# Filter pieces on GpSimd's queue and a first transform with eight column groups ahead, in a frequency filter followed by a SiLU layer

## Chip, core and metric

The kernel runs on one core of one Trainium2 chip. The metric is the device time of one execution in microseconds (us); all times below are in us unless marked ns. An execution is also taken by the hardware profiler, and the profile's times are counted from the start of its span.

## What is computed

A batch of 8 sequences of 3008 rows and 256 channels goes through a filter in the frequency domain, and then every row goes through two matrix multiplications with a SiLU between them.

```python
X = np.fft.rfft(x, axis=1)                      # x: 8 x 3008 x 256
Y = X * (filt_r + 1j * filt_i)[None, :, :]      # 1505 frequencies x 256
y = np.fft.irfft(Y, n=x.shape[1], axis=1)       # 8 x 3008 x 256
h = y.reshape(24064, 256) @ w_in                # w_in: 256 x 2048
out = (h / (1 + np.exp(-h))) @ w_out            # w_out: 2048 x 256
```

The weights of the two layers come as 64-bit floating point numbers and are turned into 32-bit ones on the chip.

## The kernel before

**Transforms.** A sequence of 3008 = 94 x 32 rows is transformed in steps: a first transform over the 94 rows that lie 32 apart (as matmuls with the table `wx_t`), a second over the remaining 32 with twiddle factors (tables `d_t`), the product with the filter (`f_t`), an inverse second transform (tables `e_t` and `minus`), a trip to DRAM and back that regroups the rows (tensors `d2`, tile `t4`), and the inverse first transform, the third stage (`stage3`, table `wi_t`). Its result `y` feeds the layers.

**Layers.** The 24064 rows are worked off in 48 pairs of row blocks; each pair has 8 steps over blocks of 256 hidden units. A step does seven matmuls for the first layer (`hidden`, tiles px and pyz, L750) and seven for the second (`project`, tile acc, L813), in place of eight each, with VectorE building the sums that this saving needs. The transforms of the later sequences are placed between these steps by a list of due times (`put`, `pending`). That part is not touched by the change.

**The start-up.** The first sequence (`part = spectral(0)`) has nothing to hide behind. Its instructions are written out by hand in program order (L1053 to L1164), each engine works off its own instructions in that order, and waits follow from the tiles that are read and written. The pieces that the change and the prediction's steps touch are these.

- `idle` (L1039) and `idle_wide` (L1045) issue matmuls whose result nobody reads. `idle(48)` at L1053 is TensorE's first work. `idle_wide(14)` at L1154 stands between the second sequence's first-transform matmuls and `stage3` of the first sequence.
- Every fp32 matmul shows as two records in the profile.
- `load_first` (L281) issues three loads of x on SP's queue: rows 0 to 11 of each group of 32, rows 12 to 23 (both into the memory of `w_t`, as `place`), rows 24 to 31 (into `x_all`).
- `stage1_first(k, i)` (L295) multiplies column group k (16 of the 256 channels). Before, i = 0 covers rows 0 to 23 (384 columns of the moving operand) and i = 1 rows 24 to 31 (128 columns). After i = 1 a VectorE transpose (L304) moves the group's result from its PSUM tile pa into SBUF. L1092 to L1097 order the sixteen groups: four groups' first pieces ahead, then in turn the second piece of group k and the first piece of group k + 4.
- `bank` (L251) hands out PSUM tiles in this part in a cycle of eight: two of pool `fps`, four of `accps`, two of `xps`. A tile that is handed out anew is written once its earlier readers are done.
- `forward` (L446, second transform, tile pb), `multiply` (L465, VectorE, L479), `add` (L484, GpSimd), `inverse_first` (L506, tile pc, L522) and `rows_first` (L526, copies to q and writes to DRAM d) follow, for six groups g. `load_t4_rows` (L561) reads them back; `stage3` (L568, tile pd, L580) multiplies.
- `load_filters(queues, first, last)` (L235) issues sixteen loads of pieces of the filter, eight on each of two queues: first 4 of 12 slices (64 KB each), then the other 8 (128 KB each). At L1065 and L1068 both parts go to SP's and ACT's queues.
- `weights(j)` (L1003, `load_weights` at L898) issues two loads of 256 KB of weight block j on SP's queue. `bits`, `converted`, `rounded` and `placed` turn a block into 32-bit numbers on VectorE and ScalarE.
- `second["load_x"](u, nc.gpsimd)` at L1115 issues two loads of the second sequence into `x_all` on GpSimd's queue; `second["stage1"]` (L335) reads them after the first sequence's inverse matmuls.

The bank's turn is the one thing that a sentence can't say:

```python
early[0] += 1
k = early[0] % 8
if k < 2:
    return fps.tile([128, 2, C], FP32, name=name, tag="f")
if k > 5:
    return xps.tile([128, 2, C], FP32, name=name, tag="x" if k == 6 else "yz")
return accps.tile([128, 2, C], FP32, name=name, tag=f"a{k - 2}")
```

Of the kernel before, what the change touches and what calls it, by code (L numbers as in the profile page):

```python
# [56 lines left out]
NS, NG = 24, 6  # L57
# [21 lines left out]
def slot_residue(g, bank, j):  # L79

    s = 2 * g + bank
    return (s, 47 - s, s + 12, 35 - s)[j]
# [88 lines left out]
def kernel(  # L171
# [9 lines left out]
    nc = tc.nc  # L181
# [39 lines left out]
    wx_t = cpool.tile([96, 128], FP32)  # L221
# [9 lines left out]
    gate = cpool.tile([128, 1], FP32)  # L231
    x_all = xpool.tile([128, 2, 2, 2 * C], FP32)
    x_t = [x_all[:, i] for i in range(2)]

    def load_filters(queues, first, last):  # L235

        for j in (0, 2, 1, 3):
            s0, tau = slot_residue(0, 0, j), (1 if j % 2 == 0 else -1)
            for half in range(2):
                off, t = (s0, tau) if half == 0 else (94 - s0, -tau)  # L240
                for k, filt in enumerate((filt_r, filt_i)):
                    queues[j // 2].dma_start(
                        out=f_t[k][32 * j + half:32 * j + 32:2].rearrange("p g k c -> p (g k) c")[:, first:last],
                        in_=bass.AP(tensor=filt.tensor, offset=filt.offset + (off + t * first) * C,
                                    ap=[[94 * C, 16], [t * C, last - first], [1, C]]))
# [5 lines left out]
    def bank(b, name, spare=None):  # L251


        if early[0] is None and spare in ("x", "yz"):
            return xps.tile([128, 2, C], FP32, name=name, tag=spare)
        if early[0] is None and spare is not None:
            return accps.tile([128, 2, C], FP32, name=name, tag=f"a{spare}")
        if early[0] is None:
# [9 lines that stand above are left out]
    def spectral(b):  # L268
# [4 lines left out]
        xs, us, t2s, banks, prods, halves, t4s = {}, {}, {}, {}, {}, {}, {}  # L273

        def load_rows(view, u, n, queue=None):

            (queue or nc.sync).dma_start(out=view[0:96],
                              in_=bass.AP(tensor=x.tensor, offset=x.offset + (b * S + 4 * u) * C,
                                          ap=[[32 * C, 96], [1, 4 * n * C]]))
# [15 lines left out]
        def stage1_first(k, i):  # L295

            if i == 0:
                banks[k] = bank(b, f"pa_{b}_{k}").rearrange("p a c -> p (a c)").rearrange(
                    "p (n c) -> p n c", c=16)
            n0, n = ((0, 24), (24, 8))[i]  # L300
            nc.tensor.matmul(out=banks[k][:, n0:n0 + n], lhsT=wx_t, rhs=xs[i][0:96, :, 16 * k:16 * k + 16],
                             start=True, stop=True)
            if i == 1:
                nc.vector.transpose(out=us["t2"][:, :, 16 * k:16 * k + 16].rearrange("p s c t -> p c s t"),  # L304
                                    in_=banks.pop(k).rearrange("p (s t) c -> p c s t", t=2))

        def load_x(u, queue=None):


            xs[u] = x_t[u % 2]  # L310
            if b == 1:
                xs[u] = xs[u].rearrange("p a n -> p (a n)")
                return load_rows(xs[u], u, 1, queue)
            for h in range(2):
                for r0, nr in ((0, 32), (32, N1 - 32)):
                    nc.sync.dma_start(
                        out=xs[u][64 * h + r0:64 * h + r0 + nr],
                        in_=bass.AP(tensor=x.tensor,
                                    offset=x.offset + (b * S + 32 * r0 + 4 * u + 2 * h) * C,
                                    ap=[[32 * C, nr], [32 * N1 * C, 2], [1, 2 * C]]))  # L320

        def sums(u):
            ut = x_t[0] if u == 7 else upool.tile([128, 2, 512], FP32, name=f"u_{b}_{u}", tag="u")
            xt = xs.pop(u)
            for par, op in ((0, ALU.add), (1, ALU.subtract)):
                nc.vector.tensor_tensor(out=ut[0:111, par], in0=xt[0:111, 0], in1=xt[0:111, 1], op=op)
            us[u] = ut
# [268 lines left out]
        def evict_y(g, h):  # L596
# [2 lines left out]
            copy = nc.scalar.copy if h else nc.vector.tensor_copy  # L599
            copy(out=dst[:, :, h, :, n0:n0 + 4], in_=us["pd", g][h].rearrange("p a i n -> p a n i"))  # L600

        return dict(us=us, store_rows=store_rows, evict_y=evict_y, evict_t1=evict_t1, halves=halves, load_first=load_first, stage1_first=stage1_first, load_x=load_x, sums=sums, stage1=stage1, reverse_x=reverse_x,
                    load_fold=load_fold, fold=fold, stage1_fold=stage1_fold, evict_fold=evict_fold,
                    load_t2=load_t2, forward=forward, multiply=multiply, add=add, inverse=inverse, inverse_first=inverse_first, rows_first=rows_first, even=even, rows=rows, load_t4=load_t4, load_t4_rows=load_t4_rows, stage3=stage3)

# [111 lines left out]
    v, gp = nc.vector, nc.gpsimd  # L717
# [180 lines left out]
    def load_weights(j, queue=None):  # L898

        if j in (8, 11, 12, 13):  # L900
            pool, tag = (t4pool, "t4") if j in (11, 12) else (upool, "u")
            raw = pool.tile([128, 2, 512], U32, name=f"raw_{j}", tag=tag)
        else:

            if j in (0, 2):
                t = ypool.tile([128, 2, HALF], FP32, name=f"raw_{j}", tag="y")
                raws.setdefault("tiles", []).append(t)
                raws["at"] = t.rearrange("p a n -> p (a n)").bitcast(U32)[:, 0:2048]
                raws["y"] = raws["at"]
                raws.setdefault("first", raws["at"])  # L910
            elif j == 4:
                raws["at"] = spool.tile([128, 2048], U32, name=f"raw_{j}", tag="s")
            elif j == 6:
                raws["at"] = gpool.tile([128, 2048], U32, name=f"raw_{j}", tag="g")
            elif j in (9, 14):
                raws["at"] = raws["y"]
            at = 1024 * (j in (1, 3, 5, 7, 10, 15))
            raw = raws["at"][:, at:at + 1024].rearrange("p (w n) -> p w n", w=2)
        queue = queue or nc.sync
        queue.dma_start(  # L920
            out=raw[:, 0].rearrange("p (a n) -> p a n", a=2),
            in_=moe_w_in.bitcast(U32)[:, 256 * j:256 * j + 256].rearrange("(a p) n -> p a n", p=128))
        queue.dma_start(out=raw[:, 1], in_=moe_w_out.bitcast(U32)[128 * j:128 * j + 128, :])
        raws[j] = raw
# [78 lines left out]
    def weights(*js, queue=None):  # L1003
        for j in js:
            if wide:
                load_weights(j, queue)
# [5 lines left out]
    def converted(*js):  # L1012
        if wide:
            convert_weights(*js)
# [24 lines left out]
    def idle(n, ps=None):  # L1039

        ps = (ps or bank(0, "idle")).rearrange("p a c -> p (a c)")
        for _ in range(n):
            nc.tensor.matmul(out=ps[:, 0:128], lhsT=wx_t, rhs=wx_t, start=True, stop=True)

    def idle_wide(n, ps=None, rhs=None):  # L1045

        ps = ps or bank(0, "idle")
        for _ in range(n):
            nc.tensor.matmul(out=ps[:, 0], lhsT=wx_t, rhs=wide_rows if rhs is None else rhs,
                             start=True, stop=True)  # L1050

    wide_rows = d_t[0:96].rearrange("p s r n -> p (s r n)")[:, 0:256]
    idle(48)  # L1053

    by_gpsimd = (0, 1, 2, 3, 4)
    part, second = spectral(0), spectral(1)
    weights(0, 1, 2, 3)
    place = part["load_first"]()
# [6 lines left out]
    load_filters((nc.sync, nc.scalar), 0, 4)  # L1065
    nc.scalar.dma_start(out=d_t[:, 8:16], in_=d_dram[:, 8:16])
    nc.scalar.dma_start(out=e_t[:, 0:2], in_=e_dram[:, 0:2])
    load_filters((nc.sync, nc.scalar), 4, 2 * NG)  # L1068
    nc.scalar.dma_start(out=d_t[:, 16:NS], in_=d_dram[:, 16:NS])
    nc.scalar.dma_start(out=e_t[:, 2:NG], in_=e_dram[:, 2:NG])  # L1070
    nc.sync.dma_start(out=wi_t, in_=ws_dram.ap())
    weights(4, 5)

    minus = [typool.tile([128, 4, 2, 2, 64], FP32, name=f"minus_{i}", tag="ty") for i in range(2)]
    gp.tensor_scalar(out=minus[0][:, 0:2], in0=e_t[:, 0:2], scalar1=bias_t[:, 3:4], scalar2=None, op0=ALU.mult)
# [13 lines left out]
        for i, scale in enumerate((-1.0, bias_t[:, 4:5])):  # L1089
            nc.scalar.activation(out=neg[i][:, NG - 1], in_=e_t[:, NG - 1, :, 0], func=AFT.Identity, scale=scale)  # L1090

    for k in range(4):  # L1092
        part["stage1_first"](k, 0)
    for k in range(16):
        part["stage1_first"](k, 1)
        if k < 12:
            part["stage1_first"](k + 4, 0)  # L1097
    weights(6, 7)
    part["forward"](0, fill=4)
    placed(0, 1)  # L1100
    for g in range(1, 4):
# [2 lines left out]
    def products(g):  # L1104
        for k in range(2):
            part["multiply"](g, k)
            if g in by_gpsimd:
                part["add"](g, k)
# [2 lines left out]
        part["inverse_first"](g)  # L1111
        part["rows_first"](g)

    for u in range(2):
        second["load_x"](u, nc.gpsimd)  # L1115
    products(0)
    products(1)
    inverse(0)
# [14 lines left out]
    inverse(4)  # L1133
    part["load_t4_rows"](1)
    part["load_t4_rows"](2)
    weights(8)
    converted(4, 5)
    bits(6, 7)
    placed(2, 3)
# [11 lines left out]
    gp.tensor_copy(out=gate, in_=w_t[:, 4, A11, 0, 0:1])  # L1151
    for u in range(2):
        second["store_rows"](u)
    idle_wide(14)  # L1154
    for g in range(4):
        part["stage3"](g)
    nc.sync.dma_start(out=wi_t, in_=wi_dram.ap())
# [93 lines left out]
```

## Time and profile before

| | us |
|---|---|
| median of 3 runs | 2580.01 (2579.96 to 2581.22) |
| the profiled execution | 2580.55 |
| its span | 2578.7 |
| TensorE busy in it | 2555.9 (99%) |
| VectorE busy | 1665.8 (65%) |
| ScalarE busy | 1086.0 (42%) |
| GpSimd busy | 421.3 (16%) |
| first matmul of a layer (px) starts at | 78.87 |

In the profile, PE is TensorE's matmuls, PEld its weight loads, DVE VectorE, ACT ScalarE, POOL GpSimd and SP SyncE; a q behind a name is the engine's sequencer, which issues DMAs and waits. L304 is line 304 of the kernel. `out<-in` names the tiles written and read. A timeline row gives start, duration, engine, line, operation, tiles, the count of merged instructions and, in brackets, how long the engine had been idle before it and what ended that. The granted clock is 1.00 when TensorE may run at full speed and 0.50 at half.

### The profile page before, as it was taken

What the parts mean: (1) busy time and instruction counts of PE and PEld (TensorE: products, weight loads), DVE (VectorE), ACT (ScalarE), POOL (GpSimd) and SP (SyncE); (2) the same over time, 40 slices, a digit from 0 to 9 for tenths busy, and PEclk for the clock granted to TensorE, in tenths of its full rate; (3) what the DMA queues carried; (4) which work ended last, traced back from release to release, by engine and by line L of the source; (5) the groups of instructions that cost most, each with busy time, mean ns of one, the idle gap of its engine ahead of it and who ended that gap; (6) DMA issues with size and microseconds to landing.
All of it is one profiled execution on the core that took longest, in us unless ns stands there. A gap on an engine that the chain in (4) does not pass through costs nothing.

```text
span 2578.7 us, 48117 instructions
## 1 busy us (share of the span) xinstructions
PE 2555.9 (99%) x18852; PEld 2196.2 (85%) x18852; DVE 1665.8 (65%) x3588; ACT 1086.0 (42%) x3010; POOL 421.3 (16%) x670
## 2 busy tenths in 40 slices
PE   8999999999999999999999999999999999999998
PEld 6788888888888888888888888988888888888987
DVE  7866666666666666666666666666666666555554
ACT  3544444444444444434444434444444444444443
POOL 2211111121112111311122111211121112101101
PEclk9899999999999999999999999999999999999999
DMA  8621232222222222222223222331232311210011
GB/s 277 171 62 50 71 79 63 60 64 75 60 63 69 70 62 58 76 73 64 64 59 88 51 66 58 80 80 46 66 79 65 74 42 28 64 19 16 9 17 16
DMA packets 200443, 171.08 MB, mean 66 GB/s; under 512 B 122100, under 2 KB 174180, under 8 KB 199428
## 3 DMA queue, kind: packets, MB, share of 16 engines
q1 hardware_dynamic: 179000, 117.32, 19.8%
q0 software_dynamic: 16992, 44.91, 5.5%
q10 hardware_dynamic: 4224, 5.77, 0.8%
q8 instruction: 148, 2.42, 0.4%
q14 instruction: 79, 0.65, 0.1%
HBM read 96.07 MB, written 81.26 MB: 69 GB/s over the span
## 4 chain that ended last, share of the span: by engine, by line
PE 97%; DVE 1%; DMA 1%; ACT 0%; issue 0%; SPq 0%; DVEq 0%; ACTq 0%
PE acc L813 44%; PE px L750 26%; PE pyz L750 19%; PE pd L580 3%; PE pb L457 2%; PE pc L500 2%; PE pf L424 1%; PE pc L522 0%; PE pa L344 0%; PE pa L335 0%; DMA d<-q 0%; DMA t<-d 0%; DMA raw<-in_moe_w_in_dram 0%; DVE g L721 0%; DVE w_t L721 0%
## 5 line engine op out<-in xcount | busy, mean ns | idle before, releaser
L813 PE MATMUL acc<-g,w_t 128*128 128x256 f32 (+1 forms) x5376 | 1509.2, 375 | 0.4 <-DVE g L721 0.4
L813 PEld LDWEIGHTS acc<-g,w_t 128*128 128x128 f32 x5376 | 1021.6, 190 | 115.8 <-DVE g L721 0.8
L721 DVE TENSOR_TENSOR g<-pyz,abc 128x256 f32<-128x256 f32 (+1 forms) x1152 | 479.9, 417 | 620.3 <-ACT abc L771 356.0
L721 DVE TENSOR_TENSOR g<-g 128x256 f32<-128x256 f32 (+3 forms) x1152 | 599.4, 520 | 196.7 <-ACT g L754 183.6
L750 PE MATMUL px<-ty,w_t 128*128 128x256 f32 (+1 forms) x2304 | 678.3, 376 | 1.4 <-ACT abc L765 1.0
L754 ACT ACTIVATE g<-g 128x256 f32<-128x256 f32 (+1 forms) x1152 | 472.9, 411 | 250.9 <-DVE g L721 250.9
L750 PEld LDWEIGHTS px<-ty,w_t 128*128 128x128 f32 x2304 | 432.3, 190 | 64.9 <-issue 6.2
L721 POOL TENSOR_TENSOR s<-s 128x256 f32<-128x256 f32 (+1 forms) x329 | 254.8, 792 | 1416.6 <-DVE s L833 1350.6
L750 PE MATMUL pyz<-y,w_t 128*128 128x256 f32 (+1 forms) x1536 | 454.3, 378 | 0.4 <-DVE g L721 0.4
L750 PEld LDWEIGHTS pyz<-y,w_t 128*128 128x128 f32 x1536 | 283.9, 190 | 48.2 <-DVE g L721 7.9
L765 ACT COPY abc<-px 128x256 f32<-128x256 f32 (+1 forms) x384 | 141.3, 368 | 372.8 <-PE px L750 372.8
L771 ACT COPY abc<-px 128x256 f32<-128x256 f32 (+1 forms) x384 | 141.5, 368 | 338.1 <-PE px L750 337.1
L754 ACT ACTIVATE g<-px 128x256 f32<-128x256 f32 (+1 forms) x384 | 145.8, 380 | 300.2 <-PE px L750 300.1
L750 PE MATMUL px<-y,w_t 128*128 128x256 f32 (+1 forms) x768 | 232.7, 385 | 0.8 <-DVE y L594 0.8
L750 PE MATMUL pyz<-ty,w_t 128*128 128x256 f32 (+1 forms) x768 | 225.4, 375 | 0.2 <-DVE g L721 0.2
L750 PEld LDWEIGHTS px<-y,w_t 128*128 128x128 f32 x768 | 140.6, 190 | 32.9 <-DVE y L600 5.8
L750 PEld LDWEIGHTS pyz<-ty,w_t 128*128 128x128 f32 x768 | 144.6, 190 | 18.7 <-DVE g L721 1.0
L758 ACT COPY abc<-px 128x256 f32<-128x256 f32 (+1 forms) x384 | 135.3, 352 | 53.7 <-PE px L750 53.6
L580 PEld LDWEIGHTS pd<-wi_t,t 48*64 48x64 f32 x3840 | 61.3, 135 | 26.2 <-ACT g L754 16.4
L436 POOL DMA_DIRECT2D d<-tf x144 | 71.4, 503 | 30.7 <-DVE tf L432 26.7
L863 DVE STREAM_TRANSPOSE o<-s 128x256 f32<-128x256 f32 x192 | 73.9, 423 | 1.5 <-issue 0.7
L833 ACT COPY s<-acc 128x512 f32<-128x512 f32 (+1 forms) x94 | 54.2, 577 | 47.6 <-PE acc L813 47.5
(137 smaller groups left out, 1262.4 us busy)
## 6 DMA issues: line engine op xcount, KB each, us to landing
t<-d SPq DMA_DIRECT2D x120, 192.0 KB
t<-d SPq DMA_DIRECT2D x84, 256.0 KB
d<-q POOLq DMA_DIRECT2D x84, 256.0 KB, 2.6
out_dram<-o SPq DMA_DIRECT2D x636, 32.0 KB
d<-tf POOLq DMA_DIRECT2D x144, 96.0 KB, 3.3
xr<-in_x_dram SPq DMA_DIRECT2D x6, 1472.0 KB
x_all<-in_x_dram SPq DMA_DIRECT2D x72, 96.0 KB
x_all<-xr SPq DMA_DIRECT2D x72, 96.0 KB
```

What stands on the lines that cost most here:

```text
L436: nc.gpsimd.dma_start(out=d1[k // 2, :, k % 2, n0:n0 + 4], in_=us["tf"][32 * k:32 * k + NS].rearrange("p q n c -> p (q n) c"))
L457: nc.tensor.matmul(out=ps[k][32 * j:32 * j + 32, ri, :], lhsT=d_t[rows, 4 * g + at, ri, :], rhs=rhs, start=True, stop=True)
L580: nc.tensor.matmul(out=ps[h][c0:c0 + 64, cb, i, :], lhsT=t4[rows, i, 128 * cb + c0:128 * cb + c0 + 64], rhs=wi_t[rows, :], start=True, sto ...
L721: eng.tensor_tensor(out=out, in0=in0, in1=in1, op=op)
L750: nc.tensor.matmul(out=out, lhsT=w_t[:, jp, c, 0], rhs=rhs, start=start, stop=True, skip_group_check=True)
L754: nc.scalar.activation(out=g[:, k, 0:n], in_=g[:, k, 0:n] if src is None else src, func=AFT.Silu)
L758: nc.scalar.copy(out=sums[:, 0, 0:n], in_=xo)
L765: nc.scalar.copy(out=sums[:, 1, 0:n], in_=xo)
L771: nc.scalar.copy(out=sums[:, 2, 0:n], in_=xo)
L813: nc.tensor.matmul(out=acc[pair][i][:, h, 0:n], lhsT=w_t[:, jp, c, 1], rhs=g[:, k, 0:n], start=(jp == 0 and h == 0), stop=last, skip_group ...
L833: copy(out=s[:, 2 * i:2 * i + 2, 0:n], in_=acc[pair][i][:, :, 0:n])
L863: v.transpose(out=o[:, :, h, :], in_=results[pair][:, ((2, 6), (4, 1))[chunk][h], :])
```

## The change

The diff has six parts. `idle(48)` becomes `idle(27)` and `idle_wide(14)` becomes `idle_wide(16)`. The second part of the filter's loads goes to GpSimd's queue, behind a one-element GpSimd copy that reads the end of the second x piece. Weight blocks 4 to 7 are loaded in one row on SP's queue behind the filters' first part; block 8 is loaded before the second transform and no longer after `load_t4_rows`. The first transform takes three row pieces (12, 12 and 8 rows: 192, 192 and 128 columns) and does the first two pieces of eight groups ahead in place of four; then in turn the third piece of group k and the first two of group k + 8. The second sequence's two x loads become one, twice as long, on SP's queue, placed behind the first transform.

```diff
-            n0, n = ((0, 24), (24, 8))[i]
-            nc.tensor.matmul(out=banks[k][:, n0:n0 + n], lhsT=wx_t, rhs=xs[i][0:96, :, 16 * k:16 * k + 16],
-                             start=True, stop=True)
-            if i == 1:
+            n0, n = ((0, 12), (12, 12), (24, 8))[i]
+            rhs = xs[i // 2][0:96, n0 % 24:n0 % 24 + n, 16 * k:16 * k + 16]
+            nc.tensor.matmul(out=banks[k][:, n0:n0 + n], lhsT=wx_t, rhs=rhs, start=True, stop=True)
+            if i == 2:
                 nc.vector.transpose(out=us["t2"][:, :, 16 * k:16 * k + 16].rearrange("p s c t -> p c s t"),
                                     in_=banks.pop(k).rearrange("p (s t) c -> p c s t", t=2))
...
+        def load_two():
+
+            load_rows(x_all.rearrange("p i a n -> p (i a n)"), 0, 2)
+            for u in range(2):
+                xs[u] = x_t[u].rearrange("p a n -> p (a n)")
...
-    idle(48)
+    idle(27)
...
-    load_filters((nc.sync, nc.scalar), 4, 2 * NG)
+    gp.tensor_copy(out=gate, in_=place[:, 6143:6144])
+    load_filters((nc.gpsimd, nc.gpsimd), 4, 2 * NG)
...
-    weights(4, 5)
+    weights(4, 5, 6, 7)
...
-    for k in range(4):
-        part["stage1_first"](k, 0)
+    for i in range(2):
+        for k in range(8):
+            part["stage1_first"](k, i)
     for k in range(16):
-        part["stage1_first"](k, 1)
-        if k < 12:
-            part["stage1_first"](k + 4, 0)
-    weights(6, 7)
+        part["stage1_first"](k, 2)
+        if k < 8:
+            for i in range(2):
+                part["stage1_first"](k + 8, i)
+    second["load_two"]()
+    weights(8)
     part["forward"](0, fill=4)
...
-    for u in range(2):
-        second["load_x"](u, nc.gpsimd)
     products(0)
...
-    weights(8)
     converted(4, 5)
...
-    idle_wide(14)
+    idle_wide(16)
```

More of the change, by code (lines that the diff above doesn't have):

```diff
@@ L600, in evict_y @@
             copy(out=dst[:, :, h, :, n0:n0 + 4], in_=us["pd", g][h].rearrange("p a i n -> p a n i"))
-        return dict(us=us, store_rows=store_rows, evict_y=evict_y, evict_t1=evict_t1, halves=halves, load_first=load_first, stage1_first=stage1_first, load_x=load_x, sums=sums, stage1=stage1, reverse_x=reverse_x,
+        return dict(us=us, store_rows=store_rows, evict_y=evict_y, evict_t1=evict_t1, halves=halves, load_first=load_first, stage1_first=stage1_first, load_x=load_x, load_two=load_two, sums=sums, stage1=stage1, reverse_x=reverse_x,
                     load_fold=load_fold, fold=fold, stage1_fold=stage1_fold, evict_fold=evict_fold,
```

## The prediction

> **What bounds the kernel now.** I read the page first: busy times, and the shares of the chain that ended last.
>
> ```profile
> PE 2555.9 (99%) x18852; PEld 2196.2 (85%) x18852; DVE 1665.8 (65%) x3588; ACT 1086.0 (42%) x3010; POOL 421.3 (16%) x670
> PE 97%; DVE 1%; DMA 1%; ACT 0%; issue 0%; SPq 0%; DVEq 0%; ACTq 0%
> ```
>
> TensorE is the bound of the kernel, and the diff changes nothing that TensorE does in the layers. What it changes lies ahead of the first layer matmul, at 78.87. So the question is only how far that instant moves: everything after it follows one for one.
>
> The chain of waits up to there is next (start, us, what):
>
> ```profile
> 42.71 1.80 DVE w_t L479 x3
> 50.22 8.87 PE pc L522 x160
> 59.88 6.31 DMA d<-q
> 67.53 3.78 DMA raw<-in_moe_w_in_dram
> 71.33 6.82 PE pd L580 x254
> 78.87 1.19 PE px L750 x2
> ```
>
> It is one string: VectorE's filter products, the inverse matmuls, a write to DRAM (d) and back (the row named raw covers the last load of t4, issued at 66.89 to 67.49), the third transform (pd), the first layer. The list begins at 42.71. The timeline shows what stands ahead of it (start, us, engine, line, out<-in):
>
> ```profile
> 17.92 2.82 PE L301 MATMUL pa<-w_t,wx_t 96*128 96x384 f32 x8
> 21.11 0.49 PE L301 MATMUL pa<-x_all,wx_t 96*128 96x128 f32 x2 [0.38 <-DMA x_all<-in_x_dram]
> 21.44 0.81 PE L301 MATMUL pa<-w_t,wx_t 96*128 96x384 f32 x2
> 22.09 0.38 PE L301 MATMUL pa<-x_all,wx_t 96*128 96x128 f32 x2
> 22.51 0.72 DVE L304 STREAM_TRANSPOSE w_t<-pa 128x512 f32<-128x512 f32 x1 [0.15 <-PE pa L301]
> 32.06 2.51 DVE L304 STREAM_TRANSPOSE w_t<-pa 128x512 f32<-128x512 f32 x4 [0.15 <-PE pa L301]
> 34.50 1.39 DVE L980 TENSOR_TENSOR w_t<-scratch 128x256 f32<-128x256 f32 x4
> ```
>
> Two records are one fp32 matmul. Four column groups are multiplied ahead; then each group costs TensorE 0.87 (22.51 to the next transpose at 23.38), and VectorE waits 0.15 for each. Only the last four transposes run at VectorE's own pace, (2.51-0.72)/3 = 0.60. The last ends at 34.57; the second transform begins at 34.63, and from 34.50 VectorE has no gap until 45.7. So 34.57 is on the path: what moves it moves the end.
>
> Last, the table by stretches with the granted clock (stretch: length, PE, PEld, DVE, ACT, POOL busy, clock, DMA share, GB/s):
>
> ```profile
> 44.42:47.84 3.42, 3.21 (x44) 1.91 (x48) 2.28 (x5) 1.38 (x3) 3.42 (x6) 0.50 1.06 381
> 71.72:75.13 3.41, 3.41 (x143) 3.41 (x136) 1.34 (x3) 1.85 (x4) 0.00 (x0) 0.50 0.46 163
> 81.96:85.38 3.42, 1.85 (x6) 0.63 (x5) 3.35 (x9) 2.16 (x6) 0.00 (x0) 1.00 0.99 331
> 85.38:88.80 3.42, 3.17 (x8) 2.54 (x9) 1.98 (x5) 1.44 (x4) 0.00 (x0) 0.50 1.08 365
> ```
>
> The clock halves after thin stretches: after TensorE's gap to 44.60, after the one before 71.33 (half until 81.96), and after 81.96 to 85.38, which had six 256-column records of 0.215, some 38% of it.
>
> [...] The trace has SP and ACT issuing filter pieces every 0.6 us.
>
> **The change, part by part.**
>
> *Eight groups ahead.* The sixteen matmuls ahead have 192 columns each, half of a 384-column one (22.09-21.44 = 0.65), so 0.33. Idle matmuls stop after 54 records instead of 96, at about 11.6 (39 records by 9.9 at the slow pace that the trace shows there, 15 more at 0.11). The first x piece lands near 14: queue SP had moved 3.56 MB by 12.0 and the piece ends at 3.67 MB; the second would by the same count end at 15.9 and was waited for until 17.8, so 1.9 is added. Eight matmuls (2.6) then end before 17.8, eight more before 20.5, under the wait for the third piece (21.11). They are free, and save 4 x 0.65 of TensorE's time later.
>
> But nine groups don't fit eight banks. Group 8 takes the bank of group 0, and in TensorE's order its two matmuls stand straight behind group 0's third piece and ahead of group 1's. Before, four groups lay between. Now (8, pieces 0 and 1) waits for transpose 0, and transpose 1 waits for (1, piece 2), queued behind them. TensorE and VectorE alternate, eight times: transpose 0.72; to TensorE 0.06 (34.57 to 34.63); weight load exposed after a wait 0.11 (21.44-21.11 = 0.33 against 22.31-22.09 = 0.22 in the stream); two 192-column matmuls 0.65; the third piece until its transpose starts 0.42 (22.51-22.09). Sum 1.96, against 0.87 before; 1.85 if the weight load hides.
>
> Transpose 0 starts at 21.64 as before. Transpose 8 starts at 21.64 + 8 x 1.96 = 37.3. The rest has only short matmuls ahead (0.22) and goes at 0.60: 7 x 0.60 + 0.72 = 4.9. End 42.2, against 34.57: **+7.7** (6.8 with 1.85). What follows shifts with it: placed(0, 1), products, inverse matmuls, the DRAM round trip.
>
> *Filters' second part on GpSimd.* Eight issues leave SP, eight leave ACT (about 0.6 each, 5 us a queue); a copy and sixteen 128 KB issues join POOL from 17.8. Two POOL issues of x_all took 1.29, so 10.3 at 0.65 and at most 21 at twice that: done by 28 to 39, then minus (1.56), then the adds, first needed at 37.24 + 7.7 = 44.9. Cover: POOL's idle time. If it goes, at most 1 us. Products of group 2 need the data near 48; the trace's POOL loads landed in 8.5 at most. Its first transfers overlap the third x piece's last microsecond: 0 to +1.0; I take 0.
>
> *Weights 4 to 7 earlier, 8 before the second transform.* No queue waits for them. Before, bits(4, 5) ran at 54.54, long after they landed. Block 8's two issues leave SP's stretch at 67.53, behind the last t4 load, so they never delayed it: 0 to -0.5, taken 0. VectorE's wait for block 8 (1.1 at 72.82) goes, and what is late next is still pd: 0.
>
> *Second batch's x by SP.* One issue replaces POOL's two (1.29 of idle POOL). It waits for the last first-transform matmul, near 39; behind it on SP stand block 8 and then the d write that was issued at 54.65, itself shifted. Its reader ran at 58.95. Cover over 15 us: 0.
>
> *Idle 14 to 16.* Two more wide matmuls are 4 records of 0.216, 0.86, inside the gap of 2.63 (68.70 to 71.33): direct cost 0. The gap becomes 1.77, which may keep the clock full. The third transform took 6.82; four full-clock groups of 1.08 (the chain's later rows of 64) are 4.32. So up to -2.5, and up to another -1.5 of the half-clock 3.1 us to 81.96. From 0 to -4.0; I take 0, since the trace shows no gap of 1.8[...].
>
> *Clock in the alternation.* TensorE streams 0.86 of each 1.96, 44%. The trace shows 38% followed by half clock and nothing between that and well-filled stretches. If halved, 0.86 is added to each turn: 0 to +6.9; I take 0 and keep a mixed +3.4 as a rival. The half-clock stretch at 44.42 may come out shorter or longer by 1.7.
>
> **Sum.** The profiled execution took 2580.55 (span 2578.7, 1.85 around it), 0.54 above the median of 2580.01. 2580.55 + 7.7 = 2588.25, or 2587.7 from the median: I say 2588.
>
> **Rivals.** *Cold alternation* (0.23): half the turns at half clock, 2588 + 3.4 = 2591.4, up to 2595 at all turns. For it: 44% lies near the 38% that went cold; against: the eight third pieces and the fill matmuls are dense after it. *The two idle matmuls pay it back* (0.17): the clock stays full through pd and the first layer steps, -2.5 to -4.0, so 2585.5 to 2584; it decides once it saves over 2.8, and then the result is no slower than can be measured. For it: clock rows above[...]. *No alternation* (0.08): if a ninth bank's wait were not there, eight groups would go at 0.87 and eight at 0.60, end 33.5, -1.0; with the full clock at pd -3.5 to -5: 2579 to 2575. Against it: `bank` counts modulo eight. *Third x piece late* (0.02): +1 and more on top, 2589 and up.
>
> **Numbers.** The forecast has 0.50. About 0.2% (5.2 us) is what a measurement of this kernel can tell from no change: 2574.9 to 2585.2. Faster: half of no alternation, 0.04. Same: its other half and most of the payback, 0.04 + 0.14 = 0.18. Slower: the rest, 0.78. Range: below 2583 lie no alternation and a little of the payback, some 0.1; above 2595 the colder turns, 0.1.
>
> **What would show it.** Right: the first nine transposes start 1.9 to 2.0 apart, each with VectorE idle for about 1.2 on pa L301, and pa waiting for transposes on TensorE; the last ends near 42; the first px shifts by as much. Wrong: transposes 0.87 apart, or 2.8 (half clock); pd in 4.3 instead of 6.8; a first transpose after 22.

## The result, and the profile after

The changed kernel takes 2588.09 us (median of 6 runs, 2587.28 to 2593.67), against 2579.99 (6 runs, 2578.14 to 2581.22) for the kernel before beside it: a ratio of 1.0036, 95% interval 1.0023 to 1.0049, so it is slower by 8.1. Forecast were 2588.0 and +7.7. The number came out; the sum behind it did not. Two of its terms were wrong by about as much as each other, with opposite signs, so that the agreement of the totals is luck, and the profile shows both.

First the page's busy times and the shares of the chain that ended last.

```profile
PE 2560.6 (99%) x18846; PEld 2202.4 (85%) x18846; DVE 1664.0 (64%) x3588; ACT 1085.6 (42%) x3010; POOL 429.2 (17%) x685
PE 97%; DMA 1%; DVE 1%; ACT 0%; issue 0%; SPq 0%; POOL 0%; DVEq 0%; ACTq 0%
```

TensorE bounds the kernel as before, with 4.7 more busy time for six records fewer: the same kind of work at a lower clock (granted 0.993 on the mean, 0.996 before). Next, the chain up to the first layer matmul (start, us, what).

```profile
40.02 5.07 PE pa L302 x20
45.08 3.10 PE pb L456 x8
...
60.27 8.86 PE pc L528 x160
...
69.94 6.48 DMA d<-q
...
77.85 3.65 DMA raw<-in_moe_w_in_dram
81.51 5.25 PE pd L586 x237
```

From the inverse matmuls (pc) on it is the same string as before, later, and the first transform (pa, L302) now stands in front of it. The alternation is seen in VectorE's transposes of the changed kernel, on the timeline (start, us, engine, line, operation, tiles, count, in brackets the idle time before and its end).

```profile
20.53 0.72 DVE L304 STREAM_TRANSPOSE w_t<-pa 128x512 f32<-128x512 f32 x1 [4.88 <-PE pa L302]
22.48 0.72 DVE L304 STREAM_TRANSPOSE w_t<-pa 128x512 f32<-128x512 f32 x1 [1.23 <-PE pa L302]
...
27.71 0.72 DVE L304 STREAM_TRANSPOSE w_t<-pa 128x512 f32<-128x512 f32 x1 [2.17 <-PE pa L302]
...
42.13 4.90 DVE L304 STREAM_TRANSPOSE w_t<-pa 128x512 f32<-128x512 f32 x8 [2.17 <-PE pa L302]
```

In each turn TensorE in its turn waits for a transpose, as here for the one that began at 27.71:

```profile
28.48 1.65 PE L302 MATMUL pa<-w_t,wx_t 96*128 96x192 f32 x4 [0.81 <-DVE w_t L304]
```

The first turn takes 22.48 - 20.53 = 1.95. From the third on a turn takes 2.89 (0.72 + 2.17). After eight turns the rest goes in 4.90, and the last transpose ends at 47.03. The granted clock stands in the table by stretches of the changed kernel, cut within 0.1 of the instants at which the clock changed, or in steps of 3.41 or 3.42 from there (stretch: length, PE, PEld, DVE, ACT, POOL busy, clock, DMA share, GB/s).

```profile
20.50:23.92 3.42, 1.81 (x10) 1.62 (x11) 1.43 (x2) 0.00 (x0) 2.22 (x5) 0.99 1.04 241
23.92:27.33 3.41, 2.60 (x10) 2.31 (x8) 0.72 (x1) 0.00 (x0) 2.26 (x5) 0.50 1.06 218
...
40.98:44.40 3.42, 3.42 (x17) 3.42 (x16) 2.27 (x4) 0.00 (x0) 0.00 (x0) 0.50 0.45 152
44.40:47.81 3.41, 3.41 (x12) 2.83 (x10) 3.41 (x8) 0.00 (x0) 0.00 (x0) 0.51 0.57 135
...
78.53:81.94 3.41, 1.79 (x34) 1.24 (x35) 3.27 (x8) 0.00 (x0) 0.00 (x0) 0.99 0.94 264
81.94:85.35 3.41, 3.41 (x144) 3.41 (x139) 2.37 (x6) 2.40 (x6) 0.00 (x0) 0.51 0.04 15
...
88.77:92.18 3.41, 2.06 (x7) 0.90 (x6) 3.34 (x10) 2.19 (x5) 1.95 (x4) 0.99 0.91 228
92.18:95.59 3.41, 2.95 (x7) 1.60 (x7) 2.65 (x7) 1.06 (x3) 0.00 (x0) 0.51 1.02 354
```

The first stretch of the alternation has TensorE busy for 1.81 of 3.42, and the next is at half clock; so it stays up to 47.8 (0.50 from 23.92 to 47.80). The same pair (thin stretch, then half clock) comes at 78.53 (1.79 busy, then 0.51) and at 88.77 (2.06 busy, then 0.51).

Places on the path in the two profiled executions (us from the span's start) tell where the shift grew and shrank:

| | before | after | shift |
|---|---|---|---|
| last transpose of the first transform ends | 34.57 | 47.03 | +12.5 |
| first filter product starts | 35.87 | 49.34 | +13.5 |
| second transform (pb), group 4 starts | 44.63 | 55.03 | +10.4 |
| third transform (pd), its main block starts | 71.33 | 81.51 | +10.2 |
| first layer matmul (px) starts | 78.87 | 88.05 | +9.2 |
| second sequence's first pa among the layer steps | 91.17 | 98.83 | +7.7 |
| end of the span | 2578.7 | 2587.9 | +9.2 |

The profiled executions took 2580.55 and 2589.67, 0.6 and 1.6 above their medians, so the last row is 1.1 over the 8.1 of the medians. The shift is 12.5, not 7.7, where the prediction's sum ends; it is down to 7.7 some 50 us later, for reasons that were not in the sum, and it grows by 1.5 again up to the end; where is not shown. The rows come from one profile of each kernel. Group 4 is where most of it goes. TensorE's timeline before:

```profile
40.39 1.23 PE L522 MATMUL pc<-z,minus 64*64 64x256 f32 x15
44.63 2.08 PE L457 MATMUL pb<-w_t,d_t 64*32 64x256 f32 x32 [3.01 <-DVE w_t L479]
```

and after:

```profile
55.03 1.14 PE L463 MATMUL pb<-w_t,d_t 64*32 64x256 f32 x32
```

Before, TensorE waited 3.01 ahead of this group and then ran it at half clock (2.08; granted 0.50 from 44.60 to 46.70). After, there is no wait and the clock is full (1.14; granted 1.00 from 55 to 57): 4.0 of the shift is gone there, and some of it is spent again close by.

### The profile page after: what moved, and what is told of

Its sections match the earlier page's. It is cut to its first block, busy times and chain, and to the rows that moved or that the text cites. A ratio compares the mean times of both kernels' runs of the same rounds, so it can differ in the third digit from the quotient of the medians.

```text
span 2587.9 us, 48103 instructions
## 1 busy us (share of the span) xinstructions
PE 2560.6 (99%) x18846; PEld 2202.4 (85%) x18846; DVE 1664.0 (64%) x3588; ACT 1085.6 (42%) x3010; POOL 429.2 (17%) x685
## 4 chain that ended last, share of the span: by engine, by line
PE 97%; DMA 1%; DVE 1%; ACT 0%; issue 0%; SPq 0%; POOL 0%; DVEq 0%; ACTq 0%
PE acc L819 44%; PE px L756 26%; PE pyz L756 19%; PE pd L586 3%; PE pb L463 2%; PE pc L506 2%; PE pf L430 1%; PE pa L302 1%; DMA x_all<-in_x_dram 1%; PE pc L528 1%; PE pa L350 0%; PE pa L341 0%; DMA raw<-in_moe_w_in_dram 0%; DMA d<-q 0%; DVE w_t L304 0%
```

## Theories and experiments

**Theory.** Nine groups on eight banks cause all of the loss, in three terms: the alternation at full clock, the half clock that its thin stretches bring on, and, against them, waits of the kernel before that were for data and not for the transform, so that a later transform swallows them. **Rivals:** the filters' queue on GpSimd makes up part of the loss; the two added idle matmuls give part back; group 4 waited for VectorE, as the profile names it, and the relief has another cause.

**Seven groups ahead.** The changed kernel, with one group fewer ahead, so that group k + 7 takes a bank whose transpose began one turn earlier:

```diff
-        for k in range(8):
+        for k in range(7):
...
-        if k < 8:
+        if k < 9:
             for i in range(2):
-                part["stage1_first"](k + 8, i)
+                part["stage1_first"](k + 7, i)
```

> The changed kernel with seven groups ahead in place of eight, so that group k + 7 takes a bank whose transpose was started one turn earlier. Theory (the eighth group ahead makes TensorE and VectorE alternate on one bank): transposes 0.87 us apart for the first ten and 0.60 after, the last ending 12.2 after the first begins (changed kernel 26.5, before 12.9); with the stall of 3.0 before the second transform's group 4 also gone, 2575 to 2577. Rival (the third row piece, or filters that now share the DMA engines with x, make the stage slow): the transposes stay more than 1.9 apart and the time stays above 2585.

Measured: 2577.65 (2576.74 to 2579.98), ratio to before 0.9996 (0.9988 to 1.0005), 10.4 below the changed kernel. VectorE's timeline:

```profile
22.00 0.72 DVE L304 STREAM_TRANSPOSE w_t<-pa 128x512 f32<-128x512 f32 x1 [0.16 <-PE pa L302]
23.08 0.72 DVE L304 STREAM_TRANSPOSE w_t<-pa 128x512 f32<-128x512 f32 x1 [0.36 <-PE pa L302]
...
29.80 4.30 DVE L304 STREAM_TRANSPOSE w_t<-pa 128x512 f32<-128x512 f32 x7 [0.15 <-PE pa L302]
```

Turns of 0.87 and 1.08 in place of 1.95 to 2.89; the last transpose ends at 34.10. One spare bank takes the alternation away, and the whole loss with it. The transposes end 13.0 after the first begins, not 12.2, and the time missed its band by 0.65. GpSimd's first add came at 39.78 (before: 37.24), since its tables were late (e_t was issued at 30.82, before at 26.41); whether that is the reason is tried further below.

**The turns filled.** The changed kernel, with the next group's third piece computed three more times (the same values again) in each of seven turns, where TensorE would wait. VectorE's turn stays; what the theory takes for the clock's cause goes:

```diff
...
+        for _ in range(3 if k < 7 else 0):
+            part["repeat_third"](k + 1)
```

> The changed kernel with the next group's third piece multiplied three times more in each of the first seven turns, into the columns that its own matmul then overwrites, while TensorE would wait for the transpose. Theory (the turns are 2.9 instead of 1.95 because TensorE's idle share lets the clock go to half): all turns 1.95, granted clock 1.00 throughout, last transpose ends 20.6 after the first begins instead of 26.5, and 2581 to 2583. Rival (the clock is low for another reason, or the long turns have another cause): turns stay at 2.9, time 2588 or more.

Measured: 2582.23 (2579.70 to 2585.42), ratio 1.0012 (1.0006 to 1.0019). VectorE's timeline:

```profile
23.66 0.72 DVE L304 STREAM_TRANSPOSE w_t<-pa 128x512 f32<-128x512 f32 x1 [1.23 <-PE pa L302]
...
37.29 4.90 DVE L304 STREAM_TRANSPOSE w_t<-pa 128x512 f32<-128x512 f32 x8 [1.23 <-PE pa L302]
```

All eight turns take 1.95, (37.29 - 21.71)/8, with the clock at 1.00 from 21.70 to 37.30 (TensorE busy 13.81 of 15.60), and the last transpose ends at 42.19. This is the prediction's picture to the tenth (1.96 and 42.2), and it costs 3.0, not 7.7. What the filling gained is the price of the half clock: 2588.09 - 2582.23 = 5.9, or 5.1 from each one's distance to the kernel before beside it. More work on TensorE made the kernel faster.

**The transform alone, and all but the transform.** The kernel before with only the diff's transform part and `idle(27)`; and the changed kernel with the transform of before and `idle(48)`, of which this is the order of the groups:

```diff
...
-    for i in range(2):
-        for k in range(8):
-            part["stage1_first"](k, i)
+    for k in range(4):
+        part["stage1_first"](k, 0)
     for k in range(16):
-        part["stage1_first"](k, 2)
-        if k < 8:
-            for i in range(2):
-                part["stage1_first"](k + 8, i)
+        part["stage1_first"](k, 1)
+        if k < 12:
+            part["stage1_first"](k + 4, 0)
```

> The kernel before with only the first transform's part of the change (three row pieces, eight groups ahead, 27 idle matmuls). Theory: the alternation with half clock appears alone, last transpose 26 after the first, and 2588 as in the changed kernel, since the table has landed long before the later group 4 needs it, so that its wait absorbs 3 of the shift here too. Rival (the other parts give back what is missing between 12.5 and 8): 2590 to 2592.

> The changed kernel with the first transform of before (two row pieces, four groups ahead, 48 idle matmuls); all other parts of the change stay. Theory A (the other parts are worth nothing, as the prediction had it): 2580. Theory B (moving the filters off ScalarE's queue lets the table of the second transform's last groups land in time, so the wait of 3.0 before group 4 goes and with it a half-clock stretch): 2576, group 4's first matmul 8 after the last transpose instead of 10.

Measured: the transform alone 2589.06 (2587.14 to 2590.88), ratio 1.0041 (1.0029 to 1.0054); all but the transform 2579.31 (2577.20 to 2581.37), ratio 1.0002 (0.9994 to 1.0010). The transform part gives the whole loss. With it alone, on the old queues, group 4's wait is gone too (it starts at 55.41 with none), so the later transform swallows it without the new queues. The rest of the change sums to nothing, but not because its parts do nothing: with the old transform and the new queues, the first add of GpSimd came 2.1 later than before (39.32), and group 4 ran with no wait.

**Filters on GpSimd alone.** The kernel before, with the filters' second part on GpSimd's queue and nothing else:

```diff
-    load_filters((nc.sync, nc.scalar), 4, 2 * NG)
+    gp.tensor_copy(out=gate, in_=place[:, 6143:6144])
+    load_filters((nc.gpsimd, nc.gpsimd), 4, 2 * NG)
```

> The kernel before with only the filter's second part moved to GpSimd's queue, behind the one-element copy. Theory (the move has two effects of opposite sign: the table lands in time for group 4, but GpSimd's minus, which waits for e_t behind the slower first filters, delays GpSimd's adds by 2): first add near 39.3 instead of 37.2, no 3.0 wait ahead of group 4, and no change within 1.5 us. Rival (covered by GpSimd's idle time, as the prediction had it): first add at 37.2.

Measured: 2583.21 (2580.23 to 2586.07), ratio 1.0016 (1.0009 to 1.0023), 3.7 slower where at most 1.5 was expected. The profiled execution is the slowest of the 18 (2586.07), so what it shows may be larger than in most. GpSimd's timeline in it:

```profile
39.40 1.56 POOL L1076 TENSOR_SCALAR minus<-e_t,bias_t 128x512 f32<-128x512 f32 x1 [9.78 <-DMA e_t<-e_tbl]
40.93 1.08 POOL L277 DMA_DIRECT2D x_all<-in_x_dram  x2
42.02 0.74 POOL L487 TENSOR_TENSOR z<-z,p 128x256 f32<-128x256 f32 x1
```

The filters' own issues end at 29.6 and are not what is late. GpSimd then waits 9.78 for the table e_t, and its two x loads stand between that and the first add, which comes at 42.02, 4.8 later than before. TensorE's inverse matmuls wait for it:

```profile
42.82 1.11 PE L522 MATMUL pc<-z,e_t 64*64 64x256 f32 x2 [3.63 <-POOL z L487]
```

The table is late because its issue on ScalarE's queue is. Before:

```profile
26.41 0.44 ACTq L1067 DMA_DIRECT2D e_t<-e_tbl  x1
```

and in this kernel, where it is issued 5.4 later and GpSimd's wait for it ends 7.6 after that:

```profile
31.84 0.33 ACTq L1067 DMA_DIRECT2D e_t<-e_tbl  x1
```

In the changed kernel it is issued at 30.91, and GpSimd's wait ends at 37.30.

In the change the second sequence's x stands on SP's queue, so its 1.08 is not ahead of the adds; that, the weights' place and the idle matmuls are all that this kernel lacks against the one with all but the transform, which was 3.9 faster. Which of them gives how much was not tried.

**Group 4's wait.** The profile names VectorE (w_t L479). The kernel before, with the third part of the table d_t, which group 4 multiplies by, issued ahead of the filters' second part on ScalarE's queue:

```diff
-    load_filters((nc.sync, nc.scalar), 4, 2 * NG)
     nc.scalar.dma_start(out=d_t[:, 16:NS], in_=d_dram[:, 16:NS])
+    load_filters((nc.sync, nc.scalar), 4, 2 * NG)
```

> The kernel before with one load moved: the last third of the second transform's table (d_t, slots 16 to 23) goes to ScalarE's queue ahead of the filter's second part instead of behind it. Theory (TensorE's wait of 3.0 ahead of group 4 is for that table, not for VectorE's product as the profile names it): no such wait, group 4 starts right behind the first inverse matmuls, 7.5 to 8.5 after the last transpose instead of 10.1, and 1 to 3 us less than before. Rival (the wait is for VectorE): it stays at 3.0 and the time within 1 us of before.

Measured: 2580.91 (2577.82 to 2583.74), ratio 1.0005 (0.9997 to 1.0013): no gain, a miss. But TensorE's timeline answers the question:

```profile
40.79 1.11 PE L457 MATMUL pb<-w_t,d_t 64*32 64x256 f32 x20
43.01 0.67 PE L457 MATMUL pb<-w_t,d_t 64*32 64x256 f32 x12 [1.12 <-issue]
45.44 2.74 PE L522 MATMUL pc<-z,e_t 64*64 64x256 f32 x14 [1.75 <-DVE w_t L479]
```

and so does VectorE's:

```profile
43.98 3.70 DVE L479 TENSOR_TENSOR w_t<-pb,filt 128x512 f32<-128x512 f32 x6 [4.00 <-DMA raw<-in_moe_w_in_dram]
```

With the table early, group 4 starts at 40.79, right behind the matmuls ahead of it, and all of it runs before the first of VectorE's w_t products begins at 43.98. So the wait of 3.01 was not for those products but for the DMA (in the kernel before, the table's issue stands behind the filters', at 36.20). The time moved on: VectorE now waits 4.00 for a DMA ahead of its w_t products, and TensorE 1.75 for VectorE. The row names another tile's load; what those products read by DMA is the filter, whose pieces now stand behind the table, so it is most likely these that are late, which was not tried by itself. An earlier load here made another later.

**Seven ahead with the first table early.** To get GpSimd's adds back in time, seven ahead with e_t's first part issued right behind d_t's first part, and the same with 20 idle matmuls ahead of pd in place of 16:

```diff
...
     nc.scalar.dma_start(out=d_t[:, 0:8], in_=d_dram[:, 0:8])
+    nc.scalar.dma_start(out=e_t[:, 0:2], in_=e_dram[:, 0:2])
     load_filters((nc.sync, nc.scalar), 0, 4)
     nc.scalar.dma_start(out=d_t[:, 8:16], in_=d_dram[:, 8:16])
-    nc.scalar.dma_start(out=e_t[:, 0:2], in_=e_dram[:, 0:2])
...
-    idle_wide(16)
+    idle_wide(20)
```

> The changed kernel with seven groups ahead, and the first third of e_t loaded before the filter's first part on ScalarE's queue instead of behind it. Theory: GpSimd's adds start with the first products again (near 36.8 instead of 39.8 in the version with seven ahead), the inverse matmuls 2 earlier, and 2575 to 2576, under both kernels. Rival (the filter's first part or the table d_t is then late, or the d write and its way back set the end): no less than the 2577.65 of seven ahead.

> The same with 20 wide idle matmuls ahead of the third transform instead of 16. Theory (a gap ahead of the third transform costs 2.5 to 4[...]): the third transform always takes about 4.3 and the spread of the times shrinks; 0 to 2 less than with 16. Rival (its small matmuls let the clock go anyway, or the idle matmuls reach into the third transform's start): the same or up to 1 more.

Measured: 2577.61 (2575.15 to 2578.83), ratio 0.9994 (0.9986 to 1.0002); with 20 idle matmuls 2577.47 (2576.99 to 2578.71), ratio 0.9994 (0.9985 to 1.0002). The first add came back to 37.07, and no time came of it, so the late adds were not what kept seven ahead from its band. TensorE's timeline of the first of the two:

```profile
38.21 2.09 PE L463 MATMUL pb<-w_t,d_t 64*32 64x256 f32 x64 [1.88 <-DMA d_t<-d_tbl]
```

The second part of d_t is late in its turn. With 20 idle matmuls the third transform took 5.15 and not 4.3 (with 16: 5.17); the times spread over 1.7 in place of 3.7, and the median did not move. These two are the lowest medians of all, 1.9 and 2.0 below the kernel before, and their intervals still reach 1.

**Seven ahead with the old filter queues.** The changed kernel with seven groups ahead, and:

```diff
...
-    gp.tensor_copy(out=gate, in_=place[:, 6143:6144])
-    load_filters((nc.gpsimd, nc.gpsimd), 4, 2 * NG)
+    load_filters((nc.sync, nc.scalar), 4, 2 * NG)
```

> Seven groups ahead, with the filters' second part back on the queues of SyncE and ScalarE, and the other parts of the change kept. Theory A (GpSimd's queue is what the change loses beside the bank: its issues and the tables behind them make the first add late): the first add comes near 37 in place of 39.8 and the time is 2575 to 2577, 0.5 to 2.5 below seven ahead with the filters on GpSimd (2577.65). Theory B (the filters' bytes set it, whichever queue issues them): no change, 2577.2 to 2578.2. Above 2579 both are wrong and GpSimd's queue was a gain.

Measured: 2578.67 (2575.51 to 2581.57), ratio 0.9998 (0.9990 to 1.0006). Theory A is out, since nothing was gained; the time lies 0.5 above Theory B's band and below the mark for a gain of GpSimd's queue. With the banks right, the queue of the filters decides nothing that these runs can tell.

**Without the two added idle matmuls.** The changed kernel with `idle_wide(14)`:

```diff
-    idle_wide(16)
+    idle_wide(14)
```

> The changed kernel with the two added idle matmuls ahead of the third transform taken out again (14 in place of 16). Theory A (they give part of the shift back: the third transform took 5.8 in place of 6.8 in the changed kernel, and the first layer steps 1.5 less): without them the third transform is back near 6.8 and the time is 1 to 2.5 above the changed kernel, 2589 to 2590.5. Theory B[...]: the third transform stays within 0.5 of 5.8 and the time is 2587.5 to 2588.5.

Measured: 2589.95 (2587.97 to 2591.06), ratio 1.0042 (1.0028 to 1.0056); the changed kernel's 1.0036 lies inside that interval, so the times alone don't tell the two apart. The profile does. The third transform in TensorE's timeline of the changed kernel:

```profile
81.51 5.75 PE L586 MATMUL pd<-wi_t,w_t 48*64 48x47 f32 x254 [1.02 <-DMA raw<-in_moe_w_in_dram]
```

and without the two:

```profile
82.65 7.07 PE L586 MATMUL pd<-wi_t,w_t 48*64 48x47 f32 x254 [1.34 <-DMA raw<-in_moe_w_in_dram]
```

In the stretch from 78.30 to 81.70 TensorE was then busy for 1.17 and not for 1.78, and the granted clock, 0.88 in that stretch, was 0.50 from 81.70 to 91.90 and 0.62 from there to 95.30; the changed kernel had 1.00, then 0.52 (81.70 to 85.10), 0.97, 1.00 and 0.53 (91.90 to 95.30). From the inverse matmuls (60.58 against 60.27) to px (90.50 against 88.05) it lost 2.1. The time and the third transform are what Theory A said, but the other profiles speak against the count as the only cause: with 14 the third transform took 5.43 in the transform alone and 5.23 with the table first, and with 16 it took 7.07 in seven ahead with the old filter queues. What else has a part is not shown. Whether the 2.1 belong to the two matmuls stays open.

## Why the prediction was right, and where it was not

- **Eight groups on eight banks make eight turns: right.** A turn was put at 1.96 and takes 1.95 at full clock. Pieces one and two were free as said (they ended before the third piece landed at 20.00), and the last eight transposes took 4.90 as said. That one bank too few is the cause is shown by seven groups ahead.
- **"I take 0 and keep a mixed +3.4 as a rival": the failed step.** The clock fell in the second turn (at 23.9) and stayed at half for 23.9 (0.50 up to 47.8). The transposes' end came 4.8 later than put (+12.5 against +7.7), although in this profile they began 1.1 earlier (20.53, not 21.64), the first product another 1.0, because the fill matmuls (3.10) were at half clock too (0.51 from 44.40 to 47.81); in the end the term is worth 5.1 to 5.9. The trace of before had the warning: its stretch with six records of 0.215 was followed by half clock (0.50), and 44% streaming is nearer to that than to any well-filled stretch. In the profile's own measure the two are alike: TensorE is busy for 1.85 in that stretch and for 1.81 in the first stretch of the alternation. "The eight third pieces and the fill matmuls are dense after it" was no argument: they ran at half clock as well (0.50 from 40.98 to 44.40, 0.51 up to 47.81).
- **"What follows shifts with it": the other failed step.** It held only while nothing on the path waited for something that the transform doesn't release. Group 4 waited for a table's DMA; in the changed kernel that wait of 3.01 and the half-clock group behind it went when the transform came later. With the turns filled, +7.6 at the last transpose was +6.9 at pd (78.19), +5.3 at px (84.12), +4.1 at the end of the span and +3.0 in the medians (the profiled execution was 2.3 above its own). There the shift went elsewhere: a pause of 1.92 ahead of group 4, for which the profile names no wait, and half clock in that group (1.96, against 1.13 of the next; granted 0.80 on the mean from 52 to 60) took the relief back, and the third transform took 5.06 in place of 6.8. So a full-clock alternation was mis-sized by 4.7, whose parts are not all shown, and the clock by 5 to 6 the other way: 7.7 is their near cancellation, by luck, and 8.1 was measured.
- **Filters' second part, "if it goes, at most 1 us": mis-sized.** The issues ended at 28.4, inside the 28 to 39, and the adds were covered by the late transform. Where that cover is gone, the adds come 2.1 to 4.8 late, and alone this part costs 3.7 (with the other parts of the change, but not the transform, nothing); the step that was overlooked is the tables' place behind the filters on ScalarE's queue. In this change it cost nothing, as taken.
- **Weights and second x: 0, not contradicted.** All but the transform sums to +0.1 (0.9994 to 1.0010), with the filters' cost and these in it.
- **Idle 14 to 16, "from 0 to -4.0; I take 0": open.** One pair of profiles puts it near -2, inside the range that was given, but the third transform's time did not follow the count in the others. The rival's condition, that it saves over 2.8 and makes the result no slower than can be measured, was not met.
- **Half-clock stretch at 44.42, ±1.7:** it was not there any more; its 1.0 on group 4 is in the relief above.

## What to carry to other kernels

Count the groups that are worked ahead against the banks: with eight ahead on eight banks, the next group had no bank until a transpose was done, and two engines that overlapped began to alternate (a turn of 1.95 to 2.89 in place of 0.87); with seven ahead they overlapped again (0.87 and 1.08). Price a wait of TensorE twice, once as time and once as the clock of what follows it (here about 3 and 5). Before a shift is carried through to the end, ask of each wait on the path whether the thing shifted releases it: a wait for a load can swallow a shift (here one of 3.01), and the engine that the profile names need not be the one that came last (here VectorE was named and a table's load was it).

## What the runs showed of the hardware

- In the changed kernel half clock came after stretches in which TensorE was busy for more than half of the time: those with 1.79, 1.81 and 2.06 of 3.41 or 3.42 busy were each followed by it (0.51, 0.50, 0.51), and one with 2.58 (85.35 to 88.77) was followed by full clock (0.99). The busy time alone doesn't settle it: in seven ahead with the first table early, TensorE stood idle for 1.33 ahead of 34.27 and for 1.88 ahead of 38.21, was busy for 4.85 of the 7.00 from 34.00 to 41.00, and the clock was 1.00 there and up to 72.00.
- The clock came back after stretches of different length and filling. The third transform filled the stretch from 81.94 to 85.35 (3.41 busy at 0.51), and the next was at 1.00; at the end of the alternation TensorE was full from 40.98 to 47.81 (6.83 busy at 0.50 and 0.51) before the clock was 1.00; the stretch from 92.18 to 95.59, with 2.95 busy at 0.51, was followed by 1.00; and in the kernel before the third transform filled the stretch from 71.72 to 75.13 (3.41 busy at 0.50), and the clock stayed at half until 81.96. Why is open.
- No gain of the filters' move to GpSimd's queue, with its issues of 0.51 to 0.68, is shown: alone it was 3.7 slower, and with seven ahead 2577.65 (ratio to before 0.9988 to 1.0005) stands against 2578.67 (0.9990 to 1.0006) on the old queues. It also moved another queue's issues: ScalarE's queue has the same issues ahead of the table e_t in both kernels (the eight that it lost stood behind), and yet e_t was issued at 26.41 before and at 30.91 after. With the filters on the old queues it came at 25.37 with the table first; with them on GpSimd's it came at 30.82 in seven ahead, at 30.67 in all but the transform and at 31.84 in filters alone. By what way is not shown.
